# Adding all fourteen w2 blocks to x in one go, with moved ones columns and key copies, in a fused attention and feed-forward kernel

## The chip, the cores and the metric

The kernel runs on one core of a Trainium2 chip. The metric is the device time of one execution in microseconds (us). Each execution is labelled fast or slow. For a single-core program "slow" means more than 1.5% above that kernel's fastest execution in the same set. Where I quote a median it is of all runs of that set, unless I say otherwise.

A trace has PE (TensorE matmuls), PEld (its weight loads), DVE (VectorE), ACT (ScalarE), POOL (GpSimd) and SP (SyncE, which issues most transfers; SPq is its queue). L followed by a number is a line of that kernel's source, so the same instruction has slightly different line numbers in different kernels.

## The reference

A layer norm feeds two branches, and x and both branches are added:

```python
x = A_x                                  # (1, 2048, 512) bf16
xn = _layernorm(x)
# A: 32 heads of 16, four segments of 512 rows. Per segment s:
#    p = softmax(q k^T / 4 + mask);  a_dot = p v
#    a_mem = (phi(q) M) / (phi(q) z + 1e-6)      M, z: sums over the earlier segments
#    o = g * a_mem + (1 - g) * a_dot;  M += phi(k)^T v;  z += sum phi(k)
# then  A = o @ wo
# B: silu(xn @ w1) @ w2                  # inner width 1792 = 14 blocks of 128
return x + A + B
```

## The kernel before

The program is recorded by a small scheduler in Python. It keeps a clock of estimated TensorE time and calls the parts of the work as generators. In the traces the matmuls of TensorE and the instructions of VectorE come in just the order that it builds; below, "the built order" is the order of instructions on each engine in the built program. The skeleton is 80 score tiles: 4 segments s, 4 blocks dt of 8 heads, 5 tiles (q0 to q4) each. A score tile is a group of small matmuls into the single score buffer psS, followed by one exp over 128 x 2048 on ScalarE, which writes Pt:

```python
psS = psatt.tile([P, 4, L], F32, name="psS")        # one buffer
...                                                  # 4 or 8 small matmuls per tile
nc.scalar.activation(out=Pt[:], in_=psS[:], func=AF.Exp, scale=SCALE)
```

Between two score tiles TensorE gets about ten 512-column matmuls of filler: projections k, q, v; blocks h of the hidden layer (w1), whose tanh runs on ScalarE and whose product runs on VectorE; products with w2; and products with wo. The part that the change rewrites splits the 14 w2 blocks into 7 and 7:

```python
FA = 7
def first_fill(s, st):                 # first 7 blocks of w2, added to x
    for j in range(TPS):
        while st.get("nh", 0) < FA or (s > 0 and sts[s - 1].get("outs", 0) <= j):
            yield
        psA = pp.tile([P, L], F32, name="psA", tag="ps")
        w2_part(st, j, psA[:, :], range(0, FA), FA - 1)
        acc = segp.tile([P, D], F32, name="acc", bufs=TPS)
        nc.vector.scalar_tensor_tensor(out=acc[:], in0=psA[:, :], scalar=0.5,
            in1=x_sb[:, s * TPS + j, :], op0=ALU.mult, op1=ALU.add)
        ...
def out_fill(s, st):                   # last 7 blocks of w2 and wo, in one PSUM bank
    for j in range(TPS):
        ...
        psO = pp.tile([P, L], F32, name="psO", tag="ps")
        w2_part(st, j, psO[:, :], range(FA, FT), None)
        yield
        while st.get("normed", 0) < DT:      # attention output of segment s normalised
            yield
        wo_part(s, st, j, psO[:, :])         # 4 matmuls, then o_t = psO * 0.5 + acc, store
        ...
```

Normalisation (`norm_fill`) runs per block dt: the reciprocal denominators go out to memory as `rec_d`, come back broadcast into `oT` and `Dr`, VectorE forms `Dr = phiQT * Dr` and `oT = N_sb * oT`, TensorE does one matmul `psN` with the memory, and VectorE adds. The scheduler spaces the blocks 1.0 us apart:

```python
later((6500 if s < NSEG - 1 else 3000) + 1000 * (dt - d0),
      lambda dt=dt: scale(dt, oT[:, dt, :], Dr[:, dt, :]))
```

The very last block does not make that trip. Its denominators `recg` are broadcast by four matmuls, `psRep`. Before that, for every block, `sums` sends the denominators out of the two P.V results (`No_t`, `N_t`) into `zf`, and `merge` joins the halves:

```python
nc.vector.tensor_copy(out=No_t[:], in_=psPV[:, :])      # odd heads
nc.scalar.copy(out=N_t[:], in_=psPV[:, :])              # even heads
... zf <- No_t, zf <- N_t (4 small transfers);  N_t <- No_t (4 transfers, all on SyncE's queue)
nc.vector.reciprocal(out=rec[:], in_=zf[:]);  recg = rec * gate
```

The softmax here doesn't subtract the row's maximum and nothing guards it: scores larger than these inputs give would overflow.

## Time and profile before

| | before |
|---|---|
| median of 3 runs (range) | 271.84 us (271.73 to 273.14) |
| first exp (Pt) starts | 15.08 us |
| last exp starts | 245.73 us |
| from there to the end of the span (the tail) | 24.97 us |

From the page of the kernel before: busy time and share of the span, the granted TensorE clock in tenths over 40 equal slices, the chain that ended last by engine, and the costliest group.

```profile
PE 229.3 (85%) x1879; PEld 100.9 (37%) x1912; DVE 170.9 (63%) x297; ACT 206.0 (76%) x192; POOL 128.5 (47%) x224
PEclk9869999999999999999999999999999995999999
PE 39%; ACT 22%; DVE 18%; issue 11%; POOL 5%; DMA 3%; DVEq 0%; SPq 0%; ACTq 0%; POOLq 0%
L576 ACT ACTIVATE Pt<-psS 128x2048 bf16<-128x2048 f32 x80 | 150.4, 1880 | 19.2 <-PE psS L568 15.1
```

No engine is full. The tiles run one after the other, since there is one score buffer (TensorE waits 12.9 us in total for an exp to leave it). I estimated each period as the larger of what stands on TensorE (0.216 us for a matmul of 512 columns) and what stands on ScalarE (1.88 us for an exp, 0.61 for a tanh) between two exps. So one reads *periods between exps*, and asks which are longer than the work in them. Note the clock row: it is low in slices 2 to 3 (7 to 20 us) and in slice 34 (223 to 230 us).

The start, from the timeline of the kernel before (start us, duration us, engine, line, operation; in brackets the idle time before it and what ended it):

```profile
6.70 0.71 DVE L148 TENSOR_SCALAR xn_t<-x_sb,mv_all,rstd_all 128x512 bf16<-128x512 bf16 x2
7.91 0.90 POOL L734 MEMSET V_109<- 128x960 bf16 x1
8.00 2.75 DVE L148 TENSOR_SCALAR xn_t<-x_sb,mv_all,rstd_all 128x512 bf16<-128x512 bf16 x2 [0.59 <-POOL rstd_all L143]
8.83 1.12 POOL L734 MEMSET V_110<- 128x960 bf16 x1
15.08 1.88 ACT L576 ACTIVATE Pt<-psS 128x2048 bf16<-128x2048 f32 x1
```

The first two xn_t took 0.71 us together, the next two 2.75 us, while GpSimd cleared the V tiles. The windows view (stretch, length, busy time of each engine, then granted clock, transfer share and GB/s) shows TensorE busy for 0.61 of the 2.00 us from 8 us on, and its clock at 0.51 and 0.50 in the later stretches:

```profile
8.00:10.00 2.00, 0.61 (x8) 0.43 (x7) 2.00 (x1) 0.65 (x2) 2.00 (x5) 1.00 1.06 378
11.00:12.00 1.00, 1.00 (x13) 1.00 (x11) 0.03 (x1) 0.51 (x1) 1.00 (x3) 0.51 1.03 409
15.00:16.00 1.00, 0.78 (x5) 0.40 (x4) 0.00 (x0) 1.00 (x2) 0.77 (x2) 0.50 1.06 355
```

Normalisation in segment 3, on TensorE (timeline of the kernel before). TensorE stands idle for 0.86 and 0.54 us before two psN matmuls, and what stands behind a psN in the built order starts after it. After 222 us the same 16 P.V matmuls take 1.26 us instead of 0.73; the granted clock is 1.00 up to 222.6 us and 0.50 from there to 229 us:

```profile
219.55 0.38 PE L434 MATMUL psN<-Dr,Mbf 128*128 128x512 bf16 x1 [0.86 <-DVE hT L349]
220.82 0.73 PE L642 MATMUL psPV<-Pt,V_110 128*32 128x512 bf16 x16 [0.56 <-DVE hT L349]
222.09 0.38 PE L434 MATMUL psN<-Dr,Mbf 128*128 128x512 bf16 x1 [0.54 <-DVE oT L438]
222.69 1.26 PE L642 MATMUL psPV<-Pt,V_110 128*32 128x512 bf16 x16 [0.22 <-DVE hT L349]
```

The tail, from the waits from 245 us on (who waited for whom: us in total, times, longest):

```profile
DVE oT L426 <- DMA N_sb<-No_t: 2.3, 1, 2.3
PE psRep L460 <- DVE recg L681: 2.0, 1, 2.0
DVE rec L680 <- DMA zf<-N_sb: 1.3, 1, 1.3
```

### The profile page before, as it was taken

Reading aid. Unit: us, or ns where it says so; the run is one execution under the profiler, and the core shown is the slowest. Engines: PE = TensorE matmul, PEld = TensorE weight load, DVE = VectorE, ACT = ScalarE, POOL = GpSimd, SP = SyncE. Lnnn points to the kernel's source line nnn. Section 1 sums busy time; section 2 is a strip of 40 time slices with the busy share of each in tenths; the row PEclk is TensorE's granted clock in tenths of the full one; section 3 lists DMA queues with packets and bytes.
Section 4 is the critical chain, followed back from the end, with each engine's and each line's share of the span. In section 5 each row is a group of like instructions: output and inputs, shape, how many; then the busy total and the mean of one; then the engine's idle time right before and its main releaser. Section 6 shows DMA issues by size and latency. Waiting matters only on the chain.

```text
span 270.7 us, 5102 instructions
## 1 busy us (share of the span) xinstructions
PE 229.3 (85%) x1879; PEld 100.9 (37%) x1912; DVE 170.9 (63%) x297; ACT 206.0 (76%) x192; POOL 128.5 (47%) x224
## 2 busy tenths in 40 slices
PE   6689879986979787697999887989999968998883
PEld 6533334332333343233433442434434322433341
DVE  4538557797557639898237359873355285639653
ACT  1298998887999898688799895889888975774200
POOL 3844764795732277778333655473433421333000
PEclk9869999999999999999999999999999995999999
DMA  6999123012012220124110220000111300112102
GB/s 209 387 358 251 26 42 63 5 29 42 16 31 34 51 79 12 21 58 100 41 44 10 100 76 2 13 20 13 39 34 48 117 15 6 53 62 78 42 10 78
DMA packets 28883, 18.36 MB, mean 68 GB/s; under 512 B 15162, under 2 KB 28346, under 8 KB 28858
## 3 DMA queue, kind: packets, MB, share of 16 engines
q1 hardware_dynamic: 28858, 18.03, 24.0%
q8 instruction: 15, 0.25, 0.4%
q14 instruction: 10, 0.08, 0.1%
HBM read 11.27 MB, written 2.42 MB: 51 GB/s over the span
## 4 chain that ended last, share of the span: by engine, by line
PE 39%; ACT 22%; DVE 18%; issue 11%; POOL 5%; DMA 3%; DVEq 0%; SPq 0%; ACTq 0%; POOLq 0%
ACT Pt L576 14%; PE ps L209 13%; PE psA L485 6%; PE psS L568 6%; ACT th L343 4%; PE psO L485 4%; DVE hT L349 4%; PE psO L512 2%; POOL Pt L588 2%; DVE stats L134 2%; DVE oT L426 2%; DVE Dr L423 1%; DVE rec L680 1%; PE psOt L485 1%; PE psPV L642 1%
## 5 line engine op out<-in xcount | busy, mean ns | idle before, releaser
L576 ACT ACTIVATE Pt<-psS 128x2048 bf16<-128x2048 f32 x80 | 150.4, 1880 | 19.2 <-PE psS L568 15.1
L588 POOL TENSOR_SCALAR_AFFINE_SELECT Pt<-Pt 128x512 bf16<-128x512 bf16 (+1 forms) x112 | 79.1, 719 | 90.1 <-ACT Pt L576 89.8
L349 DVE SCALAR_TENSOR_TENSOR hT<-th,ps 128x512 bf16<-128x512 bf16 x56 | 37.5, 685 | 44.4 <-ACT th L343 44.1
L209 PE MATMUL ps<-xnT,w_sb 128*128 128x512 bf16 x211 | 55.7, 388 | 4.7 <-DVE hT L349 2.8
L343 ACT ACTIVATE th<-ps 128x512 bf16<-128x512 f32 x56 | 32.6, 612 | 4.7 <-DVE hT L349 2.0
L209 PEld LDWEIGHTS <-w_sb 128*128 128x128 bf16 x224 | 20.5, 99 | 28.7 <-issue 10.3
L485 PEld LDWEIGHTS <-hT 128*128 128x128 bf16 x224 | 19.9, 98 | 26.8 <-issue 6.7
L485 PE MATMUL psA<-w_sb,hT 128*128 128x512 bf16 x109 | 28.7, 380 | 0.3 <-issue 0.2
L568 PE MATMUL psS<-qT,kT 16*128 16x512 bf16 (+3 forms) x256 | 17.5, 302 | 7.9 <-ACT Pt L576 7.7
L568 PE MATMUL psS<-qT,kTo 32*128 32x512 bf16 (+3 forms) x256 | 17.5, 304 | 6.9 <-ACT Pt L576 5.2
L485 PE MATMUL psO<-w_sb,hT 128*128 128x512 bf16 x82 | 21.4, 381 | 0.0
L221 POOL TENSOR_SCALAR ek<-ek 128x512 bf16<-128x512 bf16 x24 | 14.9, 629 | 5.1 <-ACT ek L218 5.0
L209 PE MATMUL ps<-wv_sb,xnT 128*128 128x512 bf16 x63 | 15.6, 379 | 1.9 <-DVE qT L302 1.5
L209 PE MATMUL ps<-xnT,wk_sb 128*128 128x512 bf16 x54 | 16.4, 395 | 0.5 <-issue 0.2
L568 PEld LDWEIGHTS <-kTo 32*128 32x128 bf16 x256 | 6.7, 91 | 26.5 <-issue 25.1
L209 PE MATMUL ps<-xnT,wq_sb 128*128 128x512 bf16 x57 | 15.9, 392 | 0.3
L523 DVE SCALAR_TENSOR_TENSOR o_t<-psO,acc 128x512 bf16<-128x512 f32 x12 | 8.3, 689 | 11.2 <-PE psO L512 11.1
L651 DVE CAST No_t<-psPV 128x512 bf16<-128x512 f32 x16 | 10.9, 681 | 6.9 <-PE psPV L642 6.9
L302 DVE CAST qT<-ps 128x512 bf16<-128x512 f32 x16 | 10.9, 682 | 6.4 <-PE ps L209 4.5
L500 DVE SCALAR_TENSOR_TENSOR acc<-psA,x_sb 128x512 f32<-128x512 f32 x16 | 11.0, 687 | 4.9 <-PE psA L485 3.9
L653 ACT CAST N_sb<-psPV 128x512 bf16<-128x512 f32 x16 | 9.5, 591 | 5.7 <-PE psPV L642 5.7
L568 PEld LDWEIGHTS <-kT 16*128 16x128 bf16 x256 | 6.3, 92 | 19.9 <-issue 19.8
(87 smaller groups left out, 286.4 us busy)
## 6 DMA issues: line engine op xcount, KB each, us to landing
w_sb<-in_B_w_dram SPq DMA_DIRECT2D x2, 1792.0 KB
oT<-rec_d SPq DMA_DIRECT2D x15, 128.0 KB
out_dram<-o_t SPq DMA_DIRECT2D x12, 128.0 KB
Dr<-rec_d SPq DMA_DIRECT2D x11, 128.0 KB
x_sb<-in_A_x_dram SPq DMA_DIRECT2D x1, 1024.0 KB
N_sb<-No_t SPq DMA_DIRECT2D x64, 16.0 KB
x_sb<-in_A_x_dram SPq DMA_DIRECT2D x2, 256.0 KB
wk_sb<-in_A_wk_dram SPq DMA_DIRECT2D x1, 512.0 KB
```

The lines of the kernel that those rows point to most:

```text
L209: nc.tensor.matmul(ps[:, :], lhsT=lhsTs(ki), rhs=rhss(ki), start=(ki == 0), stop=(ki == DT - 1))
L221: nc.gpsimd.tensor_scalar(out=ek[:], in0=ek[:], scalar1=1.0, scalar2=0.0, op0=ALU.min, op1=ALU.max)
L302: nc.vector.tensor_copy(out=qT[:], in_=ps[:, :])
L343: nc.scalar.activation(out=th[:], in_=ps[:, :], func=AF.Tanh, scale=0.5)
L349: nc.vector.scalar_tensor_tensor(out=hT[:], in0=th[:], scalar=1.0, in1=ps[:, :], op0=ALU.add, op1=ALU.mult)
L485: nc.tensor.matmul(psO, lhsT=st["hT"][ft][:, j * P : (j + 1) * P], rhs=w2_sb[:, ft, :], start=(ft in (0, FA)), stop=(ft == last),)
L500: nc.vector.scalar_tensor_tensor(out=acc[:], in0=psA[:, :], scalar=0.5, in1=x_sb[:, s * TPS + j, :], op0=ALU.mult, op1=ALU.add,)
L568: nc.tensor.matmul(psS[:, g, c : c + nq], lhsT=kk[r0:r1, kt * P : (kt + 1) * P], rhs=st["qT"][dt][r0:r1, kt * P : L], start=True, stop=Tru ...
L576: nc.scalar.activation(out=Pt[:], in_=psS[:], func=AF.Exp, scale=SCALE)
L588: nc.gpsimd.affine_select(out=v, in_=v, compare_op=ALU.is_ge, fill=0.0, base=0, pattern=[[0, v.shape[1]], [1, P]], channel_multiplier=-1,)
L651: nc.vector.tensor_copy(out=dst[:], in_=psPV[:, :])
L653: nc.scalar.copy(out=dst[:], in_=psPV[:, :])
```

## The change

The stated intent: move the ones columns and the key copies, and add all 14 blocks of w2 to x in fp32 in three segments, so that only wo is left for the normalised part. The diff has five parts. Its core:

```diff
# (1) V clears ("ones columns"): from after the start-up to its front
+    for i in range(2):                       # right after pm_odd
+        vts.append(cpool.tile([P, TPS, H // 2, 3, DH], BF16, name=f"V{i}"))
+        nc.gpsimd.memset(vts[i][:, :, :, 1, :], 0.0)
+        nc.gpsimd.memset(vts[i][:, :, :, 1, 0:1], 1.0)
-    for vt in vts:                           # after the start-up
-        nc.gpsimd.memset(vt[:, :, :, 1, 1:DH], 0.0)
-        nc.gpsimd.memset(vt[:, :, :, 1, 0:1], 1.0)
# (2) key copies: only the first of segment 0 stays on ScalarE (two copies each)
-        if s == 0:
+        if s == 0 and dt == 0:
# (3) w2
-FA = 7
+FA = [FT, FT, FT, 7]
-            psO = pp.tile([P, L], F32, name="psO", tag="ps")
-            w2_part(st, j, psO[:, :], range(FA, FT), None)
-            yield
             while st.get("normed", 0) < DT:
                 yield
+            psO = pp.tile([P, L], F32, name="psO", tag="ps")
             wo_part(s, st, j, psO[:, :])
-                hcount["freed"] += FT - FA
   ... (start flags, and FA[s] for FA elsewhere)
# (4) spacing of the scale steps
-            later((6500 if s < NSEG - 1 else 3000) + 1000 * (dt - d0), ...
+            later((6500 if s < NSEG - 1 else 3000) + (2400 if s < NSEG - 1 else 1000) * (dt - d0), ...
# (5) tail: last block of the last segment only ("final")
+                if final:
+                    Ne_t = work.tile([P, L], BF16, name="No_t")
+                    nc.vector.tensor_copy(out=Ne_t[:], in_=psPV[:, :])
-            for par, src in ((1, No_t), (0, N_t)):
+            for par, src in ((1, No_t), (0, Ne_t if final else N_t)):
-                nc.sync.dma_start(                                  # merge
+                (nc.scalar if final else nc.sync).dma_start(
-                st["rec"][dt] = (recg, clock["vt"] + 1500)          # when psRep may stand
+                st["rec"][dt] = (recg, clock["vt"] + 3500)
```

More of the change, by code (lines that the diff above doesn't have):

```diff
@@ L103 @@
         nc.gpsimd.memset(pm_odd[32 * g : 32 * g + 16, :], 0.0)
+    vts = []
+    for i in range(2):
+        vts.append(cpool.tile([P, TPS, H // 2, 3, DH], BF16, name=f"V{i}"))
+        nc.gpsimd.memset(vts[i][:, :, :, 1, :], 0.0)
+        nc.gpsimd.memset(vts[i][:, :, :, 1, 0:1], 1.0)
     clock = {"vt": 0.0, "n": 0, "tick": None}
@@ L234, in phi_part @@
         later(900, mn)
-    vts = []
-    for i in range(2):
-        vts.append(cpool.tile([P, TPS, H // 2, 3, DH], BF16, name=f"V{i}"))
     def start_proj(s, st):
@@ L474, in norm_fill @@
                 )
-            later((6500 if s < NSEG - 1 else 3000) + 1000 * (dt - d0), lambda dt=dt: scale(dt, oT[:, dt, :], Dr[:, dt, :]))
+            later((6500 if s < NSEG - 1 else 3000) + (2400 if s < NSEG - 1 else 1000) * (dt - d0), lambda dt=dt: scale(dt, oT[:, dt, :], Dr[:, dt, :]))
         while st["normed"] < DT:
@@ L486, in w2_part @@
                 psO, lhsT=st["hT"][ft][:, j * P : (j + 1) * P], rhs=w2_sb[:, ft, :],
-                start=(ft in (0, FA)), stop=(ft == last),
+                start=(ft in (0, FA[NSEG - 1])) if st is sts[NSEG - 1] else (ft == 0),
+                stop=(ft == last),
             )
@@ L493, in first_fill @@
         for j in range(TPS):
-            while st.get("nh", 0) < FA or (s > 0 and sts[s - 1].get("outs", 0) <= j):
+            while st.get("nh", 0) < FA[s] or (s > 0 and sts[s - 1].get("outs", 0) <= j):
                 yield
             psA = pp.tile([P, L], F32, name="psA", tag="ps")
-            w2_part(st, j, psA[:, :], range(0, FA), FA - 1)
+            w2_part(st, j, psA[:, :], range(0, FA[s]), FA[s] - 1)
             acc = segp.tile([P, D], F32, name="acc", bufs=TPS)
@@ L504, in first_fill @@
             if j == TPS - 1:
-                hcount["freed"] += FA
+                hcount["freed"] += FA[s]
             yield
@@ L513, in wo_part @@
                 psO, lhsT=st["oT"][:, dt, j * P : (j + 1) * P], rhs=wo_sb[:, dt, :],
-                start=False, stop=(dt == DT - 1),
+                start=(dt == 0 and s < NSEG - 1), stop=(dt == DT - 1),
             )
@@ L632, in pv_part @@
         last = st is sts[NSEG - 1]
+        final = last and dt == DT - 1
         if dt == 0:
@@ L896 @@
         psOs.append(pt.tile([P, L], F32, name="psOt"))
-        for ft in range(FA, FT):
+        for ft in range(FA[s], FT):
             w2_part(st, j, psOs[j][:, :], range(ft, ft + 1), None)
```

## The prediction

> **What bounds it now.** No engine is full: TensorE 85% busy, ScalarE 76% (page). The chain that ended last is PE 39%, ACT 22%, DVE 18%, issue 11%. Each of 80 score tiles costs one exp (Pt, 1.88 us in the groups, about 1.77 of slot in the timeline), and the single score buffer makes 2.43 us the shortest period seen. From the built order I counted what stands between two exps: a full filler of 10 wide matmuls plus scores is about 2.6 us of TensorE (0.216 us each at full clock); each tanh, key copy or evacuation adds 0.6 us of ScalarE. Tiles run at the larger of TensorE (2.2-2.7) and ScalarE (1.8-3.6); stalls come on top. Four places lose time:
>
> 1. Start: the third and fourth xn_t take 2.75 us together (8.00-10.75) where the first two took 0.71. GpSimd is clearing the V tiles at 7.91-10.3. [...] TensorE idles, and its clock is 0.50 from 11 to 17.6 us (windows).
> 2. First four periods: 13.6 us; each key copy pair is 1.2 us on a full ScalarE.
> 3. Normalisation in segments 2 and 3: Dr/oT products bunch on VectorE, psN matmuls wait in TensorE's queue. Periods of 4.4 and 3.7 us from 161, and 4.0, 5.5, 4.4 from 216, with the clock at 0.50 around 224-228. About 7 us above the load.
> 4. Tail, 25 us from the last scores: psRep waits 2.0 us for recg, oT 2.3 for the No_t merge, PV and psN about 2.5 more.
>
> **Changes and worth.** Total matmuls are the same (224 w2, 64 wo).
> - V clears move to 2-5 us, while GpSimd waits for statistics: xn_t back near 0.8 us; -2 us, another -1 if the clock holds.
> - Key copies of tiles 1-3 of segment 0 leave ScalarE for VectorE (0.68) and GpSimd (0.6-1.2). First four periods: load falls from 13.3 to 10.4, then TensorE-bound. Earlier h tiles give about 1.3 back. Net -2.
> - All of w2 first: filler becomes mixes of h and w2 instead of runs of h, then w2+wo. ScalarE load of the ten tiles from 75 us falls from 28.3 to 24.7. Summed maxima fall only 1-2 us over segments 1-3, because some alternation remains and the next segment's w2 waits for wo. No psO waits in PSUM for normalisation.
> - Scale spacing 2.4 us: -3 us of item 3.
> - Tail: dt 2's psN goes before the last tile, even sums come from a VectorE copy (0.68), the merge goes through ScalarE's queue, psRep stands later: -3.5 us. TensorE still has about 16 us there, plus 2 us of output DMA.
>
> Nearly all is critical, since tiles are serial. Sum about -12 us.
>
> **Predicted: 260 us, 255 to 266.5 (8 in 10).** Faster by over 2%: 0.91; within 2%: 0.07; slower: 0.02.
>
> **What would show it.** Xn_t pair under 1.2 us; first Pt near 12-13 us instead of 15.1; fifth about 5 us before 28.7; segment 1's first near 71 instead of 75.4; no period over 4.5 us in segments 2-3; tail near 21.5 us; TensorE busy share 87-89%.
>
> **What would make it wrong.** Clock still halved at start; GpSimd's remaining clears hitting xn_t; kTo late on GpSimd; norm products still bunching; long w2 runs starving ScalarE; the last exp's masks holding PV (only 11 matmuls before it).

One sentence of item 1 is cut from the record: it put the slow xn_t down to a general rule about two engines, which no run of this case shows. The trace's own figures (2.75 against 0.71 us) stand, and no term of the sum is cut: -2, -2, -1 to -2, -3 and -3.5 us make the "about -12".

## More of the kernel before

`wo_part` takes `o_t` from a ring of two buffers (`work`, bufs=2) and stores it through SyncE's queue.

## The result, and the profile after

The changed kernel took 262.63 us (median of 4, 261.31 to 264.47), against 271.93 us for the kernel before in the same rounds (median of 4). The ratio of fast runs is 0.9654, with a 95% interval of 0.9589 to 0.9719. Here and below a ratio is the mean time of one kernel's fast runs over the mean of the other's in the same rounds, so not quite the ratio of the medians that I quote. A second set gave 261.70 us (the control c_after below).

The total lies 2.6 us above the point that I predicted and well inside the range. How it comes about is another matter. (Spans are given to 0.1 us, so a tail, span minus the start of the last exp, is known to about 0.05 us.) The page of the changed kernel, the same rows:

```profile
PE 229.5 (88%) x1912; PEld 100.9 (39%) x1912; DVE 171.4 (66%) x301; ACT 201.1 (77%) x186; POOL 132.9 (51%) x227
PEclk9999999999999999999999999999999999999978
PE 31%; DVE 23%; ACT 19%; issue 12%; POOL 7%; DMA 5%; SPq 2%; DVEq 0%; ACTq 0%
L575 ACT ACTIVATE Pt<-psS 128x2048 bf16<-128x2048 f32 x80 | 150.6, 1883 | 16.4 <-PE psS L567 11.8
```

The start of the changed kernel, first the timeline, then one row of the windows. The second pair of xn_t is back at 0.73 us, and the clock stays at 1.00 from 8 to 18 us:

```profile
8.24 0.73 DVE L153 TENSOR_SCALAR xn_t<-x_sb,mv_all,rstd_all 128x512 bf16<-128x512 bf16 x2 [0.59 <-POOL eps_273 L737]
12.69 1.86 ACT L575 ACTIVATE Pt<-psS 128x2048 bf16<-128x2048 f32 x1
```

```profile
11.00:12.00 1.00, 0.22 (x6) 0.19 (x4) 0.69 (x1) 1.00 (x2) 0.00 (x0) 1.00 1.02 401
```

How far the changed kernel is ahead of the one before at the start of an exp, from the two timelines (before minus after, us):

| exp | before | after | lead |
|---|---|---|---|
| first, s0 dt0 q0 | 15.08 | 12.69 | 2.39 |
| fifth, s0 dt0 q4 | 28.70 | 23.72 | 4.98 |
| s0 dt3 q4 | 71.73 | 69.05 | 2.68 |
| s1 dt2 q0 | 104.22 | 97.79 | 6.43 |
| s2 dt2 q0 | 161.33 | 153.92 | 7.41 |
| s3 dt0 q0 | 190.24 | 181.51 | 8.73 |
| s3 dt2 q3 | 230.32 | 216.47 | 13.85 |
| s3 dt3 q2 | 240.54 | 230.87 | 9.67 |
| last, s3 dt3 q4 | 245.73 | 236.27 | 9.46 |
| end of the span | 270.7 | 261.2 | 9.5 |

Two things stand out. The lead reaches 13.9 us in segment 3 and then loses 3.3 us in one period of 5.77 us (s3 dt3 q1). And the tail takes 24.93 us, as before, where I had predicted 21.5.

The lost period, from the timeline of the changed kernel, engine by engine (VectorE, SyncE's queue, TensorE):

```profile
222.32 1.28 DVE L525 SCALAR_TENSOR_TENSOR o_t<-psO,acc 128x512 bf16<-128x512 f32 x2
228.87 1.29 DVE L525 SCALAR_TENSOR_TENSOR o_t<-psO,acc 128x512 bf16<-128x512 f32 x2 [5.27 <-DMA out_dram<-o_t]
220.43 0.57 SPq L694 DMA_DIRECT2D rec_d<-recg  x1
223.63 1.31 SPq L469 DMA_DIRECT2D Dr<-rec_d  x2
225.03 0.87 SPq L530 DMA_DIRECT2D out_dram<-o_t  x2
226.00 1.76 SPq L469 DMA_DIRECT2D oT<-rec_d  x2
229.62 0.73 PE L642 MATMUL psPV<-Pt,V_110 128*32 128x512 bf16 x16 [2.78 <-DVE o_t L525]
```

The third o_t needs a buffer that the first o_t's store must leave. That store stands in SyncE's queue behind the Dr loads, which wait until 223.63 us for rec_d to arrive. VectorE stands still for 5.27 us, with a P.V copy behind the o_t, and TensorE for 2.78 us. Of the 5.27 us, 1.4 pass before the store is issued (225.03) and 3.8 from there to the third o_t (228.87), so the wait in the queue is the smaller share, and the time from the store's issue to the freed buffer the larger. Before the change each o_t had seven w2 matmuls between it and the next, and VectorE's waits list no o_t that waits for a store.

The tail of the changed kernel: the wait that replaced psRep's (waits view), then VectorE and TensorE in the timeline, then one row of the windows:

```profile
PE psN L435 <- DVE Dr L424: 2.5, 1, 2.5
```

```profile
245.44 1.75 DVE L683 RECIPROCAL rec<-zf 128x256 f32<-128x256 bf16 x1 [2.61 <-DMA zf<-No_t]
247.49 0.42 DVE L424 TENSOR_TENSOR Dr<-phiQT,Dr 128x512 bf16<-128x512 bf16 x1
247.97 0.38 PE L435 MATMUL psN<-Dr,Mbf 128*128 128x512 bf16 x1 [2.54 <-DVE Dr L424]
250.60 1.06 PE L461 MATMUL psRep<-recg,sel_286 128*128 128x256 bf16 x4
```

```profile
250.00:253.00 3.00, 3.00 (x11) 1.41 (x10) 1.29 (x2) 0.00 (x0) 0.00 (x0) 0.57 0.00 0
```

The wait for psRep is gone, and one of 2.54 us for psN of block 2 is in its place. The Dr product that psN needs stands on VectorE behind the reciprocal of the last block, which waits for zf. The trace has them in that order: Dr, whose load was issued at 241.18 us, starts at 247.49, right behind reciprocal and recg, although VectorE was idle for 2.61 us before them. Then the clock halves, to 0.50, and psRep comes 14.3 us after the last exp instead of 12.3. (The trace has the clock at half from 249.2 to 252.6 us, while TensorE was busy; that alone is an estimated 1.7 us.) In the built order 61 matmuls other than P.V and psRep stand behind the last scores, where the kernel before had 68. At 0.216 us each, the median spacing of 512-column matmuls at clock 1.00 in both traces (0.427 at 0.50), the changed tail has an estimated 1.5 us less to do, and yet takes as long.

### The profile page after: what moved, and what is told of

It reads as the page before. It is cut to its first block, busy times and chain, and to the rows that moved or that the text cites. A ratio compares the mean times of both kernels' runs of the same rounds, so it can differ in the third digit from the quotient of the medians.

```text
span 261.2 us, 5138 instructions
## 1 busy us (share of the span) xinstructions
PE 229.5 (88%) x1912; PEld 100.9 (39%) x1912; DVE 171.4 (66%) x301; ACT 201.1 (77%) x186; POOL 132.9 (51%) x227
## 4 chain that ended last, share of the span: by engine, by line
PE 31%; DVE 23%; ACT 19%; issue 12%; POOL 7%; DMA 5%; SPq 2%; DVEq 0%; ACTq 0%
ACT Pt L575 13%; PE psA L486 10%; PE ps L214 8%; PE psS L567 5%; DVE hT L350 4%; ACT th L344 4%; PE psO L514 3%; POOL Pt L587 2%; DVE stats L139 2%; DVE rec L683 2%; DVE kT L272 2%; POOL ek L226 2%; POOL kTo L275 2%; DVE V_107 L309 2%; DVE oT L439 1%
## 5 line engine op out<-in xcount | busy, mean ns | idle before, releaser
L587 POOL TENSOR_SCALAR_AFFINE_SELECT Pt<-Pt 128x512 bf16<-128x512 bf16 (+1 forms) x112 | 81.4, 740 | 80.1 <-ACT Pt L575 79.9
L214 PE MATMUL ps<-xnT,w_sb 128*128 128x512 bf16 x224 | 57.6, 380 | 1.4 <-DVE hT L350 0.8
L486 PE MATMUL psA<-w_sb,hT 128*128 128x512 bf16 x196 | 47.7, 380 | 0.0
L486 PEld LDWEIGHTS <-hT 128*128 128x128 bf16 x224 | 20.6, 99 | 29.6 <-issue 7.6
L214 PEld LDWEIGHTS <-w_sb 128*128 128x128 bf16 x224 | 19.3, 97 | 25.9 <-issue 9.2
L226 POOL TENSOR_SCALAR ek<-ek 128x512 bf16<-128x512 bf16 x24 | 16.0, 672 | 2.6 <-ACT ek L223 2.6
L275 POOL TENSOR_SCALAR kTo<-kT,pm_odd 128x512 bf16<-128x512 bf16 x15 | 12.0, 800 | 8.0 <-DVE kT L272 6.9
L642 PE MATMUL psPV<-Pt,V_110 128*32 128x512 bf16 (+3 forms) x256 | 10.9, 301 | 3.0 <-DVE o_t L525 2.8
L139 DVE BATCH_NORM_STATS2 stats<-x_sb 128x6 f32<-128x512 bf16 x16 | 10.9, 680 | 3.7 <-DMA x_sb<-in_A_x_dram 3.7
L514 PE MATMUL psO<-wo_sb,oT 128*128 128x512 bf16 x48 | 12.5, 380 | 0.7 <-DVE hT L350 0.7
```

What stands on the lines that cost most here:

```text
L139: nc.vector.bn_stats(out=stats[:], in_=x_sb[:, s * TPS + j, :])
L214: nc.tensor.matmul(ps[:, :], lhsT=lhsTs(ki), rhs=rhss(ki), start=(ki == 0), stop=(ki == DT - 1))
L226: nc.gpsimd.tensor_scalar(out=ek[:], in0=ek[:], scalar1=1.0, scalar2=0.0, op0=ALU.min, op1=ALU.max)
L275: lambda: nc.gpsimd.tensor_scalar(out=kTo[:], in0=kT[:], scalar1=pm_odd[:, 0:1], scalar2=1.0, op0=ALU.mult, op1=ALU.mult,),
L486: nc.tensor.matmul(psO, lhsT=st["hT"][ft][:, j * P : (j + 1) * P], rhs=w2_sb[:, ft, :], start=(ft in (0, FA[NSEG - 1])) if st is sts[NSEG ...
L514: nc.tensor.matmul(psO, lhsT=st["oT"][:, dt, j * P : (j + 1) * P], rhs=wo_sb[:, dt, :], start=(dt == 0 and s < NSEG - 1), stop=(dt == DT - 1),
```

## The experiments

Twelve kernels ran, in three sets of four; each set shared one chip and the runs of the kernel before. Kernels starting with p are the kernel before with one part of the change. Kernels starting with a, b, c or t are the changed kernel as it is (c_after), or with parts taken away or things added. All twelve gave correct results. "Tail" is the span after the start of the last exp in the profiled run.

| run | what it is | median us (range), runs | before, same rounds | ratio of fast runs (95%) | first Pt | last Pt | tail |
|---|---|---|---|---|---|---|---|
| p1_start | before + V clears | 269.69 (269.24-270.38), 4 | 270.76 | 0.9953 (0.9901-1.0006) | 12.89 | 242.63 | 24.87 |
| p2_kto | before + key copies | 269.50 (267.69-270.48), 4 | 270.76 | 0.9936 (0.9868-1.0005) | 13.53 | 241.11 | 24.89 |
| p3_w2 | before + w2 | 264.79 (260.67-265.43), 4 | 270.76 | none: one fast run | 13.77 | 238.38 | 20.62 |
| p5_tail | before + tail part | 269.99 (268.82-271.22), 4 | 270.76 | 0.9965 (0.9894-1.0036) | 13.88 | 243.73 | 24.37 |
| c_after | all of the change | 261.70 (260.42-1223.37), 6 | 271.39 | 0.9641 (0.9605-0.9677) | | | |
| a7_notail | change without tail part | 262.73 (260.08-263.83), 6 | 271.39 | 0.9664 (0.9615-0.9712) | 13.29 | 239.49 | 22.11 |
| a9_nospace | change without spacing | 262.26 (261.18-264.19), 6 | 271.39 | 0.9668 (0.9628-0.9707) | 12.64 | 239.78 | 22.72 |
| a8_noboth | change without both | 260.00 (259.20-261.25), 6 | 271.39 | 0.9587 (0.9553-0.9620) | 13.35 | 237.56 | 20.54 |
| a6_o4 | change + four o_t buffers | 262.88 (258.94-263.14), 6 | 271.69 | 0.9638 (0.9568-0.9708) | 12.94 | 239.28 | 22.12 |
| t1_order | change + order in the tail | 260.70 (259.53-262.75), 6 | 271.69 | 0.9618 (0.9572-0.9665) | 12.64 | 240.53 | 20.47 |
| b1_o4_order | change + both of these | 258.95 (256.86-260.24), 6 | 271.69 | 0.9540 (0.9494-0.9586) | 12.72 | 234.81 | 21.29 |
| b2_noboth_o4 | a8 + four o_t buffers | 259.91 (258.25-262.13), 6 | 271.69 | 0.9571 (0.9524-0.9619) | 12.61 | 235.96 | 20.54 |

Where the ratio says "none", three runs of p3_w2 are labelled slow, because its fastest run is 4 us below them; all four lie below all seven runs of the kernel before (269.73 to 272.78). The profiled run of a6_o4 (263.14) is labelled slow by the same 1.5%.

Spacing alone on the kernel before could not be tried: the build ends in a deadlock. So it was judged by leaving it out.

### p1_start: the V clears alone

```diff
+        nc.gpsimd.memset(vts[i][:, :, :, 1, :], 0.0)       # at the front, as in the change
-        nc.gpsimd.memset(vt[:, :, :, 1, 1:DH], 0.0)        # after the start-up
```

> Kernel before with only the V clears moved to the front of the program. If GpSimd's clears were what held the third and fourth xn_t: the pair takes about 0.7 us instead of 2.75, first Pt at about 12.7 us instead of 15.1, granted clock 1.00 from 8 to 18 us instead of 0.50 from 11; the lead of the first Pt is kept to the end, 268.5 to 269.5 us. Rival, the start is bound by the loads or by the other clears and the clock stays halved: first Pt at 14.5 or later, over 271 us.

The mechanism is as expected: the pair takes 0.73 us, the first exp starts at 12.89 us, the clock is 1.00 in the windows at 8, 11 and 15 us. The profile's lead of 2.9 us at the fifth exp is kept to the end (3.1 us at the last). But the runs give only 1.1 us (269.69 against 270.76, just outside the 268.5 to 269.5 expected), and the interval includes 1. A likely reason is in the other kernels of this set, which have the *old* start: their first exp starts at 13.53, 13.77 and 13.88 us, not at 15.08. This is the timeline of p2_kto, with clears and xn_t as in the kernel before:

```profile
8.02 0.90 POOL L734 MEMSET V<- 128x960 bf16 x1
8.11 2.23 DVE L148 TENSOR_SCALAR xn_t<-x_sb,mv_all,rstd_all 128x512 bf16<-128x512 bf16 x2 [0.59 <-POOL rstd_all L143]
9.12 0.40 PE L160 MATMUL ptr<-ident,xn_t 128*128 128x128 bf16 x4 [0.19 <-DVE xn_t L148]
10.40 0.40 PE L160 MATMUL ptr<-ident,xn_t 128*128 128x128 bf16 x4 [0.44 <-DVE xn_t L148]
```

Here the third xn_t got in after the first clear: its transposes start at 9.12 us. In the profiled run of the kernel before both xn_t came late (transposes at 10.49 and 11.30), TensorE idled longer (busy 0.61 us of 8 to 10 us, here 1.45), and the clock halved (0.51 from 11 to 12 us, here 1.00). Beside the same four clears the pair took 2.75 us there, 2.23 here and 2.24 in p3_w2 (transposes at 9.35); what decides this the traces do not show. So the profile that I predicted from showed an unlucky start. Nine traces with the new start have their first exp at 12.61 to 13.35 us, the three others with the old one at 13.53 to 13.88: about 0.9 us apart on average. How often the 271 us runs of this set had the unlucky start is not known, since only one run of a kernel is traced.

### p2_kto: the key copies alone

```diff
-        if s == 0:
+        if s == 0 and dt == 0:
```

> Kernel before with only the key copies of tiles 1 to 3 of segment 0 moved from ScalarE to VectorE and GpSimd. If the lead that the changed kernel loses in the rest of segment 0 is given back by its earlier h tiles: here no h moves, so the fifth Pt comes 2 to 2.6 us earlier and the first Pt of segment 1 still 2 us or more earlier, 269.5 to 270 us. Rival, the copies only moved the load to VectorE and GpSimd: lead under 1 us at segment 1, 271 us or more.

The time is 269.50 us, 1.3 us below, as expected, but with an interval that includes 1. The fifth exp starts at 24.63 us; in p5_tail, which is identical up to there but for the key copies, it starts at 26.74. Taking off the 0.35 us by which p2_kto's first exp was earlier, the copies are worth about 1.8 us in the profiles. The lead of the fifth exp (4.07 us over the kernel before, 1.55 of it from the start) is 4.01 at the first exp of segment 1. So the loss in segment 0 of the changed kernel, from 4.98 to 2.68, does not come from the copies. In p3_w2, which has the old copies and the moved h tiles, the lead falls from 2.06 to -0.54 at s0 dt3 q4. The earlier h tiles take it, as the prediction had it: from the fifth exp to s0 dt3 q4 the traces of p3_w2 and of the changed kernel have 14 tanh on ScalarE, those of the kernel before and of p2_kto 10, and four of about 0.6 us each are 2.4 us. At that exp the loss is 2.3 to 2.6 us; at the first exp of segment 1 part of it is back, and the net loss is 1.4 us in the changed kernel (4.98 to 3.63) and 1.7 in p3_w2 (2.06 to 0.41), close to the predicted 1.3.

### p3_w2: the w2 part alone

```diff
-FA = 7
+FA = [FT, FT, FT, 7]                 # and the rest of part (3)
```

> Kernel before with only the w2 part: all 14 blocks added to x at once in segments 0 to 2. If mixing h and w2 is worth what segment 1 of the changed kernel shows (lead up by 2.4 us from 75 to 91) and the norm products still bunch: loses about 1.5 to 2 us in segment 0, wins 2 to 3 in segment 1, still has periods of 4 us and more near the third tile of segments 2 and 3; 269.5 to 272 us. Rival, the decoupling itself cures these stalls: no period over 4 us there, 265 to 267 us.

This part alone gives 264.79 us, 6.0 us below the kernel before, more than either theory's range said, and far more than the 1 to 2 us that the prediction gave it. Three of the four runs lie at 264.63 to 265.43, the profiled one at 260.67, so its trace is of a lucky run, and the sizes below are of that run. Even its slower runs lie 4.3 us or more below every run of the kernel before. Three places win:

- Segment 1 from 75 us: the kernel before had a period of 4.36 us at s1 dt0 q4 in a run of h tiles; here it is 2.59, and the lead rises by 2.4 us from s1 dt0 q0 to s1 dt1 q0, as in the changed kernel.
- Segment 3, dt2: the periods of 3.98, 5.52 and 4.43 us become 2.81, 3.79 and 2.73. The psN matmuls stand among fewer h tiles and don't wait. This is TensorE in p3_w2:

```profile
213.67 0.38 PE L434 MATMUL psN<-Dr,Mbf 128*128 128x512 bf16 x1
214.59 0.38 PE L434 MATMUL psN<-Dr,Mbf 128*128 128x512 bf16 x1
215.52 0.73 PE L640 MATMUL psPV<-Pt,V 128*32 128x512 bf16 x16 [0.56 <-DVE hT L349]
216.79 0.73 PE L640 MATMUL psPV<-Pt,V 128*32 128x512 bf16 x16 [0.54 <-DVE oT L438]
```

  No psN waits here, both P.V halves take 0.73 us, and the clock does not halve (0.9 or more in all slices of its page but the last).
- The tail: 20.62 us. In this built order 22 of the last w2 matmuls, and 13 matmuls of h, stand ahead of psN and psRep, and the Dr product of block 2 stands ahead of the last reciprocal, so TensorE's only sizeable wait is 0.83 us at psRep. I read that from the order and the waits; no run took the order alone without the rest. Part of it is less work: 59 matmuls other than P.V and psRep stand behind the last scores in the built order, against 68 before, an estimated 1.9 us at 0.216 us each.

In segment 2 the stall remains (4.57 and 3.29 us at s2 dt2 q1 and q2, where the kernel before had 4.35 and 3.65 at q0 and q1). The rival is half right: decoupling cures dt2 of segment 3, not segment 2. And one period gets longer: s3 dt3 q2 takes 4.18 us instead of 2.62, with a psN that waits 1.51 us for a Dr product.

### p5_tail: the tail part alone

```diff
+                    nc.vector.tensor_copy(out=Ne_t[:], in_=psPV[:, :])
+                (nc.scalar if final else nc.sync).dma_start(      # merge
+                st["rec"][dt] = (recg, clock["vt"] + 3500)
```

> Kernel before with only the tail part (even sums from a VectorE copy, merge on ScalarE's queue, psRep later). In the changed kernel the tail from the last Pt took 24.9 us, in the one before 25.0. If the wait only moved from psRep to the psN of tile 2, whose Dr product stands behind the reciprocal on VectorE: tail 24.5 to 25.5, 271.5 to 272.5 us, with a psN wait near 2.5 us. Rival, the tail part is worth 3 us and something else in the changed kernel ate it: tail near 22, 269 us.

The tail is 24.37 us and the time 269.99 us, 0.8 us below, within the scatter. psRep waits no more, and psN of block 2 waits 0.73 us for Dr. The expected wait of 2.5 us is not there, but neither is the gain of 3.5 us.

### c_after, a7_notail, a9_nospace, a8_noboth: what spacing and tail part are worth in the change

```diff
# a9 and a8: spacing back
+            later((6500 if s < NSEG - 1 else 3000) + 1000 * (dt - d0), ...
# a7 and a8: N_t for zf, merge on SyncE's queue, 1500 again
```

> The changed kernel once more, as the control on the chip of the next three. Expected 262 to 264 us, tail from the last Pt near 25 us, a period near 5.8 us at the second score tile of the last head block of segment 3 (o_t waits for out stores).

One of its six runs, the profiled one, took 1223 us: in its trace every period between exps is 10.6 to 14.7 us. Nothing in the other runs resembles it, and it is left out of the ratio; the other five lie between 260.42 and 262.63, with a median of 261.58 (261.70 counts all six). So the control has no trace to compare with, and what was expected of its tail and of the 5.8 us period stays unchecked; the trace of the changed kernel below is that of the first set.

> The changed kernel without its tail part. If the tail part only moved a wait: the same time within 1 us of the control, tail near 25 us, with the wait at psRep instead of at psN. Rival, the tail part does win what was predicted (3.5 us) and the rest of the change lost it: tail near 28 us, 3 us above the control.

> The changed kernel with the scale spacing of 1.0 us back. The prediction gave the spacing 3 us: then periods near 4.4 us come back by the third head block of segments 2 and 3 and the time is 265 to 266 us. Rival, from the w2-only run: the mixing of h and w2 had already taken most of those stalls, and the wider spacing makes o_t meet the blocked store queue: no period of 5.8 us, 260 to 262 us.

> The changed kernel without both the spacing and the tail part: V clears, key copies and w2 only. Rival as above (w2 is the whole gain of the body, spacing and tail cost): last Pt near 235 us, tail 20.6 to 22 us as in the w2-only profile, 257 to 259 us. If spacing and tail are worth what was predicted: 266 us or more.

Without the tail part: 262.73 us. Without the spacing: 262.26. Both are within the scatter of the control's 261.70. Without both: 260.00 us, with an interval (0.9553 to 0.9620) that overlaps the control's (0.9605 to 0.9677) only at its edge. So neither part shows the 3 and 3.5 us that I gave them; together they seem to cost, not gain. Of the two times written down for a8_noboth, 257 to 259 us and 266 or more, it misses the first by 1 us; for a9_nospace, 262.26 lies just above the rival's 260 to 262.

The traces show what the spacing does. In segment 2 it wins: s2 dt2 q1 falls from 4.57 us (a9, a8) to 2.45 (changed kernel, a7), the following tile rises from 3.29 to 3.71 between a9 and the changed kernel, and the five periods of s2 dt2 fall from 15.61 to 14.30 in sum. But it moves wo later. In the built order of a8 the 16 wo matmuls of segment 2 stand as 2, 10 and 4 in s3 dt2 q2 to q4; in the changed kernel as 8 and 8 in dt2 q4 and dt3 q0, right where the rec_d loads of the last segment are issued. With the spacing o_t waits 5.3 us (changed kernel) or 5.1 us (a7) for a store, without it 2.6 us (a8, a9). The periods of 5.77 and 5.58 us at s3 dt3 q1 go with it; it is 2.81 in a8 and a9.

The kernels without the spacing lose in the next period instead: s3 dt3 q2 takes 4.18 us in a8 and 6.36 in a9, where the rival had expected no period of 5.8 us. There a psN waits for a Dr product whose own loads are late. In a9 (TensorE, then VectorE):

```profile
234.34 0.39 PE L435 MATMUL psN<-Dr,Mbf 128*128 128x512 bf16 x1 [3.06 <-DVE Dr L424]
233.86 0.42 DVE L424 TENSOR_TENSOR Dr<-phiQT,Dr 128x512 bf16<-128x512 bf16 x1 [3.02 <-DMA Dr<-rec_d]
```

The four periods from s3 dt3 q0 to the last exp take 13.76 us (changed kernel) and 14.96 (a7) with the spacing, 12.16 (a8) and 15.16 (a9) without; in a7 and a9 the clock is also halved for 3.4 us of them (mean clock of the profiled runs 0.984 and 0.979, of the changed kernel 0.990). So a stall stands there either way, and these traces do not show that the o_t wait is what takes the spacing's 1.3 us back.

Both theories written down for a7 fail in part. psRep does wait again (1.70 us), yet the tail is 22.11 us and not 25; it is neither near 25 nor 28. The tail part lengthens the profiled tail both times it is added to kernels with the w2 part (22.11 to 24.93, 20.54 to 22.72; on the kernel before it took 0.6 off), while the times of a7 and the control do not differ.

### a6_o4, t1_order, b1_o4_order: taking the two new waits away

```diff
# a6_o4: xn_t's four buffers are unused by then
-            o_t = work.tile([P, D], BF16, name="o_t")
+            o_t = work.tile([P, D], BF16, name="xn_t", bufs=4) if s == NSEG - 2 else work.tile([P, D], BF16, name="o_t")
# t1_order: last reciprocal recorded later, psRep as soon as before
-                later(2400 if last else 5000, recip)
+                later((4000 if final else 2400) if last else 5000, recip)
-                st["rec"][dt] = (recg, clock["vt"] + 3500)
+                st["rec"][dt] = (recg, clock["vt"] + 1500)
```

> The changed kernel with segment 2's o_t taken from the ring of four that xn_t no longer uses, so that no o_t waits for a store. If the 5.8 us period is o_t waiting behind stores that stand in the queue after the Dr loads: that period falls to 2.8 us or less, no o_t wait in segment 3, last Pt 3 us earlier against the first Pt, 258 to 259.5 us. Rival, the stall is slack that a later wait takes back: last Pt or the end at most 1 us earlier, 261 us or more.

> The changed kernel with the last reciprocal 1.6 us later in the built order (so that tile 2's Dr product stands before it on VectorE) and psRep as soon as before. If the tail's loss is psN waiting for a Dr product behind the reciprocal: that wait (2.5 us) is gone, psRep near 11.5 us after the last Pt instead of 14.3, tail 21 to 22 us, 258.5 to 259.5 us. Rival, the tail is bound by the sums' transfers alone: tail over 24 us, 261.5 us or more.

> Both of the two edits on the changed kernel. If they remove separate waits they add up: last Pt 3 us earlier and tail 21 to 22 us, 255 to 256.5 us. If the second only hides what the first one had won: 258 us or more.

a6_o4: the o_t wait of segment 3 is gone, and the 5.77 us period is 2.81. But the time is 262.88 us: no gain. The next tile now takes 5.28 us, because the loads into oT, on the same queue, become what VectorE waits for. This is VectorE in a6_o4:

```profile
224.12 2.64 DVE L525 SCALAR_TENSOR_TENSOR xn_t<-psO,acc 128x512 bf16<-128x512 f32 x4
232.91 0.42 DVE L427 TENSOR_TENSOR oT<-N_sb,oT 128x512 bf16<-128x512 bf16 x1 [3.16 <-DMA oT<-rec_d]
```

That is the rival: a later wait took the gain. It need not do so: one of the six runs took 258.94, and in b1_o4_order, with the same o_t, the oT wait was 1.68 us.

t1_order: psRep starts 10.3 us after the last exp (14.3 in the changed kernel, 12.3 before), and the tail is 20.47 us. VectorE in t1_order, with Dr ahead of the reciprocal:

```profile
246.99 0.42 DVE L424 TENSOR_TENSOR Dr<-phiQT,Dr 128x512 bf16<-128x512 bf16 x1
248.62 1.75 DVE L683 RECIPROCAL rec<-zf 128x256 f32<-128x256 bf16 x1 [0.88 <-DMA zf<-No_t]
```

So the tail was indeed lost to an order on VectorE, not to the transfers; an estimated 1.7 of the 4.4 us between the two tails is the halved clock that followed the wait. The median is 260.70, above the 258.5 to 259.5 expected and about 1 us below the control of the other set, less than the tail's 4.4 us, and the two intervals overlap, so the runs alone show no gain. The profiled run lost the rest to a halved clock at 63 us and to a longer period at the o_t stall (6.70 us, the clock halved from 230.5 us on).

b1_o4_order: 258.95 us, the lowest of all. Its interval (0.9494 to 0.9586) lies below that of the changed kernel (0.9605 to 0.9677). Its median is 1.75 us below t1_order's and 3.9 us below a6_o4's in the same rounds; its interval overlaps both of theirs slightly (0.9572 to 0.9665 and 0.9568 to 0.9708). Expected were 255 to 256.5 if the two gains added up, so the o_t part is smaller than the 3 us that I read off one period.

### b2_noboth_o4

```diff
# a8_noboth, with a6_o4's line for o_t
```

> V clears, key copies and w2 only (no spacing, no tail part), with the four buffers for segment 2's o_t. o_t waited 2.6 us there: last Pt 1 to 2.5 us earlier than without, tail near 20.5 us, 257.5 to 259 us. If o_t's wait was hidden there: 260 us, as without.

259.91 us, equal to a8_noboth (260.00) within the scatter, so in that order the o_t wait was hidden, although the last exp starts 1.6 us earlier in the profiled run (0.7 of it from the start).

### Why equal programs differ by 3 us

The changed kernel, a7_notail, a6_o4, t1_order and b1_o4_order are the same program up to segment 3, and yet their profiles split in segment 0. TensorE idles 2.2 us before the scores at 63 us in both of the following. Windows of the changed kernel, then of t1_order:

```profile
61.00:63.00 2.00, 0.00 (x0) 0.00 (x0) 2.00 (x5) 2.00 (x2) 2.00 (x4) 1.00 0.33 66
63.00:65.00 2.00, 1.83 (x11) 0.80 (x11) 2.00 (x3) 2.00 (x4) 2.00 (x3) 1.00 0.62 123
```

```profile
61.00:63.00 2.00, 0.00 (x0) 0.00 (x0) 2.00 (x5) 2.00 (x2) 2.00 (x4) 1.00 0.33 66
63.00:65.00 2.00, 1.63 (x7) 0.60 (x8) 1.65 (x2) 2.00 (x4) 2.00 (x3) 0.56 0.63 124
```

In one the clock stays at 1.00 after the gap, in the other it halves (mean 0.56 from 63 to 65 us), and t1_order's lead at the first exp of segment 1 is 2.18 us where the changed kernel's is 3.62. a6_o4 and a7_notail slow down after the same gap too: a6_o4's clock is 0.81 from 63 to 65 us, and a7_notail's first six psA matmuls take 2.53 us, against 1.46 in the changed kernel and in b1_o4_order. So the same gap of 2.2 us cost 1.4 us in one run and nothing in another; what decides it these traces do not show. Nor did the length of a gap tell: in the tail of the changed kernel a gap of 2.54 us came before the halved clock (0.57 from 250 to 253 us), while in the kernel before the clock halved at 222.6 us with no gap over 0.86 us in front of it (TensorE's idle time from 219.2 to 222.6 us, psN waits among it, adds up to 1.6 us). So a wait of this kind had a second price in some runs and not in others, and a difference of the size of this 1.4 us can't be read from one profile.

## Why the prediction was right, and where it was not

The time, the direction and the range were right (260 predicted, 262.63 measured). The sum was right because errors cancelled: that it came so close was luck, though the direction was not. Of the other signs that the prediction named, the first exp of segment 1 (71.78 us for "near 71") and TensorE's share (88%) came as well. The parts, as the prediction put them, and what the runs showed:

| part | predicted us | measured us |
|---|---|---|
| V clears | -2, another -1 if the clock holds | -1.1 alone (270.76 to 269.69) |
| key copies, net of earlier h | -2 | -1.3 alone (270.76 to 269.50), without the h loss |
| all of w2 first | -1 to -2 | -6.0 alone (270.76 to 264.79) |
| spacing | -3 | none visible (262.26 without, 261.70 with) |
| tail part | -3.5 | -0.8 alone; none visible in the change |

- **Start: mechanism right, size off.** The pair (0.73 us), the first exp (12.69) and the fifth (23.72 against 28.70) came as predicted. The term was mis-sized, most likely because it was read from one trace with an unlucky start. The key copies shrank with it: the kernel before took 4.00 us for its first period, the three other traces with the old copies (p1_start, p3_w2, p5_tail) 3.48.
- **w2: the term that was mis-sized most, -6.0 us against -1 to -2.** I summed the larger of TensorE and ScalarE load per tile, which sees load, not waits. The gain was in waits: the h run in segment 1, the psN waits of segment 3, and the tail.
- **Spacing: the step "Scale spacing 2.4 us: -3 us of item 3" failed.** In segment 3 the w2 part had already removed the dt2 stall (p3_w2). In segment 2 the spacing shortens the stall, by 1.3 us in sum (15.61 to 14.30). That it gives this back by pushing wo into the burst where o_t waits for stores is argued, not shown: without the spacing the last block has a stall of its own. "No period over 4.5 us in segments 2-3" failed with it: 5.77 us.
- **A cost that the prediction lacked.** Taking w2 out of the psO group takes seven matmuls from between two o_t. Four o_t then meet a ring of two, and stores that stand behind loads that are not ready. That the ring is part of it is shown by a6_o4 (the wait goes); the part of the queue is read from the trace, since no run changed it. What the wait costs in time depends on what waits next.
- **Tail: the step "dt 2's psN goes before the last tile, ... psRep stands later: -3.5 us" failed.** In the built order psN of block 2 still stands in the tail, now ahead of psRep, and its Dr product stands behind the last reciprocal. The wait of 2.0 us at psRep became one of 2.5 us at psN, psRep started 2 us later after the last exp, and the tail stayed at 24.9 us. t1_order turned that order round and got a tail of 20.5 us (an estimated 1.7 us of the difference is the clock).

What stays open: how much of p3_w2's shorter tail comes from the order of the last w2 matmuls, beyond the smaller number of them; where the spacing's 1.3 us go; why the oT loads took 3.2 us of wait in a6_o4 and 1.7 in b1_o4_order; and the size of spacing on its own, since that does not build.

## What to carry to other kernels

A load model per stretch (the larger of two engines) finds balance, but it misses waits: here it gave the w2 part 1 to 2 us, and the chip 6.0. For each instruction that waits, look at what stands *in front of it* on the engine or queue that feeds it (here a Dr product behind a reciprocal, 2.54 us of TensorE, and a store behind loads, 1.4 of the 5.27 us that VectorE stood still). When work is taken from between two steps, ask what paced those steps before; a ring of two and a shared store queue were enough as long as seven matmuls stood in between (no o_t waits for a store in the trace before; 2.6 to 5.3 us of wait in the changed kernel and its variants a7, a8 and a9). And when a prediction rests on one profile, look for the parts of it that could have gone otherwise: here, more traces of the same code showed both the lucky and the unlucky start.
